# Float64 words turned into float32 with an integer add and fewer VectorE passes, in a fused attention, expert and gated feed-forward kernel

## The chip, the cores and the metric

The kernel runs on one core of one Trainium2 chip. Its time is device microseconds (us) of one launch, the median of three runs. Below, PE is the matrix engine, DVE is VectorE, ACT is ScalarE, POOL is GpSimd and SP is the engine whose queue issues the DMAs.

## The reference

Three stages follow one another, with 4 batches of 576 tokens:

```python
a = softmax(phi)                                  # (4, 8, 576, 32)
k_m, v_m = a^T k, a^T v                           # memory slots, 32 per head
attn = softmax(q k_m^T / 8) v_m                   # 8 heads of 64
x = heads side by side                            # (4, 576, 512)

out = p[e] * (relu(x @ w1[e]) @ w2[e])            # one expert e per token, 512 -> 1024 -> 512

h = relu(out @ w_in)                              # 512 -> 1024
gate = sigmoid(3-tap convolution of h along the tokens with conv_w)
result = (h * gate) @ w_out                       # 1024 -> 512
```

`w_in`, `conv_w` and `w_out` of the last stage come as float64. The host hands them over as 64-bit integers, so the kernel itself has to turn each pair of 32-bit words into one float32.

## The kernel before, in words

PE does all products as three float32 terms (high by high, high by low, low by high), so every operand is split by `split` (L144): an ACT copy (L145) writes the high part and a DVE or POOL subtraction (L146) the low part. Matmuls of this kind are written by `matmul3` (L156).

The order of the work on PE is written out by hand in `order()` (L37): per batch, 24 items, twice eight hidden tiles (`h`, matmuls into `ph`, evacuated by the ACT Relu of L599 and the DVE pass of L600) followed by four output tiles (`y`, matmuls into `py`, copied out by ACT at L650 and stored to `ydram`). Other steps hang between them: softmaxes, splits of expert weights (`wb`), the products `pv` with their split (`vh`, `vl`), routing. `ph`, `py` and others of one bank share the pool `ps1` of four banks (`bank`, L126). Only PE follows the list to the letter (`manual_schedule`, L683). The instructions of DVE, ACT and SP are put in order by a planner, which runs the program against its own estimate of times; each of these engines then takes its queue in that order and stands still when the first instruction in it has to wait.

The float64 weights go through sixteen pieces, eight of `w_in` and eight of `w_out`, of 128 partitions by 512 numbers (1024 words). `load_words` (L255) loads a piece into a tile `words` (`n0r` to `n15r`, two buffers). `narrow` (L260) takes two tiles of the tag `nar`, which has two buffers: `d` (called `nd`), which ends as the float32 result, and `t` (called `nt`), a help tile. It calls `to_f32` (L213) and then stores `nd` to `f_in` or `f_out` in device memory (L268). Only one piece is in work at a time, since its two tiles fill the tag. `narrow_next` in `order()` (L48) puts `nar.i` and behind it the load of piece i + 2 after items 4, 7, 10, 13 and 16 of batches 0 to 2, and the last after item 1 of batch 3. From batch 3 on, `f_in` is read back as the weights `wi`, and `f_out` as `wo`.

`to_f32` has two ACT passes (the absolute value of the high word into `t`, L218; the low word times 2^-52 in place, L224) and seven DVE passes: the clamp of `t` (L219), shift and mask into `nd` (L220), the top exponent bit from `t` (L221), the sign from the high word (L222), the power of two out of `nd` into `t` (L223), its product with the scaled low word (L225) and the sum (L226). L218 is kept in the order of the program against the other instructions so marked, the word loads of L258. The small table `conv_w` (24 numbers per partition) goes through the same function once (L621).

After the four batches comes `gated` (L761): per batch the products `pi` with `wi`, the convolution and the gate on DVE and ACT, and the products `po` with `wo`.

Of the kernel before, what the change touches and what calls it, by code (L numbers as in the profile page):

```python
# [6 lines left out]
F32 = mybir.dt.float32  # L7
F32R = mybir.dt.float32r
I32 = mybir.dt.int32
U32 = mybir.dt.uint32  # L10
I64 = mybir.dt.int64
AF = mybir.ActivationFunctionType
ALU = mybir.AluOpType
# [15 lines left out]
WORD_LEAST = 2.0 ** -15  # L29
WORD_MOST = float(np.array(0x47EFFFF0, np.uint32).view(np.float32))  # L30
# [82 lines left out]
def fused_kernel(tc, q, first, kv, kv_tail, phi, w1, w2, w_in, conv_w, w_out, out):  # L113
    nc = tc.nc
    wide = w_in.dtype == I64
    PSUM = bass.MemoryType.PSUM
    with (
# [92 lines left out]
        ydram = dram.tile([B, 4, 128, S], F32, name="ydram")  # L210


        def to_f32(dst, t, words, ne, first=lambda i: i):  # L213


            low, high = words[:, :, 0], words[:, :, 1]
            lowf, highf, u = low.bitcast(F32), high.bitcast(F32), dst.bitcast(I32)
            first(nc.scalar.activation(t.bitcast(F32), highf, AF.Abs))  # L218
            nc.vector.tensor_scalar(t.bitcast(F32), t.bitcast(F32), WORD_LEAST, WORD_MOST, ALU.max, ALU.min)  # L219
            nc.vector.tensor_scalar(u, t, 3, 0x3FFFFFF8, ALU.logical_shift_left, ALU.bitwise_and)  # L220
            nc.vector.scalar_tensor_tensor(u, t, 0x40000000, u, ALU.bitwise_and, ALU.bitwise_or)  # L221
            nc.vector.scalar_tensor_tensor(u, high, -0x80000000, u, ALU.bitwise_and, ALU.bitwise_or)  # L222
            nc.vector.tensor_scalar(t, u, -0x800000, None, ALU.bitwise_and)  # L223
            nc.scalar.activation(lowf, low.bitcast(U32), AF.Copy, scale=2.0 ** -52)  # L224
            ne.tensor_tensor(lowf, lowf, t.bitcast(F32), ALU.mult)  # L225
            ne.tensor_tensor(dst, dst, lowf, ALU.add)  # L226

        if wide:
            f_in = dram.tile([DM, F], F32, name="f_in")
# [4 lines left out]
        stages, staged, routed, words = [], {}, [], {}  # L234
# [13 lines left out]
        def narrow_at(i):  # L248
            if i < 8:
                at = (slice((i // 2) * 128, (i // 2) * 128 + 128), slice((i % 2) * 512, (i % 2) * 512 + 512))  # L250
                return w_in[at], f_in[at]
            at = slice((i - 8) * 128, (i - 8) * 128 + 128)
            return w_out[at, :], f_out[at, :]
# [6 lines left out]
        def narrow(i):  # L260

            if not wide:
                return
            raw = words.pop(i)
            d = fps[0].tile([128, 512], F32, tag="nar", bufs=2, name=f"nd{i}")
            t = fps[0].tile([128, 512], I32, tag="nar", bufs=2, name=f"nt{i}")
            to_f32(d, t, raw.rearrange("p (n w) -> p n w", w=2), nc.vector, tc.keep_in_program_order)
            nc.sync.dma_start(narrow_at(i)[1], d)  # L268

        def stage_w1(src, kc, name, batch=-1):  # L270
# [39 lines left out]
        def work(name, dt=F32):  # L310
            return ap.tile([128, S], dt, tag="w", bufs=5, name=name)
# [268 lines left out]
        fps = [ffn_cm.__enter__()]  # L580
# [35 lines left out]
        def conv_weights():  # L616
            dst = convw.rearrange("p k j -> p (k j)")
            if wide:
                cw_raw = work("cw_raw", I32)[:, :48]
                nc.sync.dma_start(cw_raw, conv_w.bitcast(I32))  # L620
                to_f32(dst, work("cwt", I32)[:, :24], cw_raw.rearrange("p (n w) -> p n w", w=2), nc.vector)  # L621
            else:
                nc.sync.dma_start(dst, conv_w)

# [34 lines left out]
        def gated_w(kc):  # L659
# [6 lines left out]
            "scores": scores, "gatew": gate_weights, "frow": first_row, "fcol": first_columns, "flog": first_expert, "ssoft": slot_softmax,  # L666
            "rtok": route_tokens, "rall": route_all, "rpp": route_scan, "rown": route_first, "asplit": split_attention,
            "vw": expert_vw, "vw0": lambda b: expert_vw(b, 0), "vw1": lambda b: expert_vw(b, 1), "w2": expert_w2, "nload": load_words, "nar": narrow, "win": gated_w,
            "conv": conv_weights, "close": close, "h": next_hidden, "y": next_second,
        }  # L670

# [240 lines left out]
```

## Time and profile before

| | |
|---|---|
| median of 3 runs | 458.12 us (455.39 to 459.72) |
| the profiled execution | 459.78 us |
| its span in the profile | 458.0 us, 8069 instructions |
| PE matmul busy | 418.3 us (91%) |
| PE weight loads busy | 374.8 us (82%) |
| DVE busy | 295.6 us (65%) |
| ACT busy | 222.7 us (49%) |
| POOL busy | 39.9 us (9%) |
| mean granted PE clock | 0.976 |
| mean DMA rate | 150 GB/s |

The span is cut by the profile into 40 slices; in these rows each digit is the busy share of a slice in tenths, or, for PEclk, the clock granted to PE in tenths of full speed:

```
PE   2656899998999589997999999999999999999995
DVE  2367797599865889677898767537920688057700
PEclk9996999999999979998999999999999999999999
```

Busy time of PE is modelled from the size of its matmuls, so a slice of nines need not be PE at its peak. Times below are us from the start of the span.

### The profile page before, as it was taken

The numbers are of one execution on the slowest core, as the hardware profiler recorded it, in microseconds if no ns is written. First come the engines' busy times: TensorE is split into PE (matmuls) and PEld (weight loads), VectorE is DVE, ScalarE is ACT, GpSimd is POOL, SyncE is SP. The second block draws the span as 40 slices with busy tenths as digits, with TensorE's granted clock in tenths as the row PEclk, the third lists the DMA queues.
The fourth block names the chain that finished last, engine by engine and source line by source line (L and its number), as shares of the span: only waits on it lengthen the run. The fifth ranks groups of instructions, "written<-read, shape, count | busy, mean of one in ns | idle before, by whom it ended". The sixth has DMA issues, their size and how long they took to land.

```text
span 458.0 us, 8069 instructions
## 1 busy us (share of the span) xinstructions
PE 418.3 (91%) x3202; PEld 374.8 (82%) x3203; DVE 295.6 (65%) x531; ACT 222.7 (49%) x408; POOL 39.9 (9%) x62
## 2 busy tenths in 40 slices
PE   2656899998999589997999999999999999999995
PEld 2333789977998479986999999899988998899884
DVE  2367797599865889677898767537920688057700
ACT  4235446465443543454646567157631675157511
POOL 1000000000000000000000031202420043003400
PEclk9996999999999979998999999999999999999999
DMA  8999948783595523989347100220012000100011
GB/s 251 346 336 403 359 146 295 270 260 130 189 326 167 167 83 135 355 297 390 78 163 268 41 14 3 101 92 1 0 40 76 1 2 1 69 25 1 1 72 52
DMA packets 28175, 68.77 MB, mean 150 GB/s; under 512 B 3136, under 2 KB 8000, under 8 KB 28128
## 3 DMA queue, kind: packets, MB, share of 16 engines
q1 hardware_dynamic: 28128, 68.16, 43.3%
q8 instruction: 27, 0.44, 0.4%
q14 instruction: 20, 0.16, 0.1%
HBM read 51.82 MB, written 16.33 MB: 149 GB/s over the span
## 4 chain that ended last, share of the span: by engine, by line
PE 67%; DMA 18%; DVE 10%; issue 2%; ACT 1%; SPq 1%; DVEq 0%; ACTq 0%
PE pi L156 22%; PE po L820 21%; PE py L156 14%; PE ph L156 6%; DMA f_in<-nd 4%; DMA kv<-in_kv_tail 3%; DMA f_out<-nd 3%; DMA ph<-in_phi 3%; DMA kv<-in_kv 2%; DVE wb L146 2%; DMA wb_0r<-in_w 2%; PE pk L361 1%; DMA n10r<-in_w_out 1%; DMA wa_1r<-in_w 1%; DVE vl L146 1%
## 5 line engine op out<-in xcount | busy, mean ns | idle before, releaser
L156 PEld LDWEIGHTS py<-h,wb 128*128 128x128 f32 x768 | 102.8, 188 | 8.5 <-issue 4.7
L156 PE MATMUL py<-h,wb 128*128 128x288 f32 x768 | 108.2, 298 | 1.1 <-DVE h L600 1.1
L156 PE MATMUL pi<-yh,wi 128*128 128x288 f32 x512 | 90.9, 295 | 0.0
L820 PE MATMUL po<-wo,g 128*128 128x512 f32 (+1 forms) x408 | 90.2, 377 | 0.0
L820 PEld LDWEIGHTS po<-wo,g 128*128 128x128 f32 x408 | 72.8, 188 | 13.2
L156 PEld LDWEIGHTS pi<-yh,wi 128*128 128x128 f32 x512 | 76.7, 189 | 0.9
L156 PE MATMUL ph<-att,vh 128*128 128x288 f32 x256 | 57.6, 318 | 11.4 <-ACT ys L650 6.6
L802 DVE SCALAR_TENSOR_TENSOR ct<-ht,convw,ct 128x575 f32<-128x575 f32 x32 | 29.8, 932 | 54.6 <-ACT ct L801 54.6
L156 PEld LDWEIGHTS ph<-att,vh 128*128 128x128 f32 x256 | 43.4, 201 | 17.3 <-ACT ys L650 7.1
L156 PE MATMUL pi<-yl,wi 128*128 128x288 f32 x256 | 54.9, 296 | 0.0
L786 POOL CAST tail<-g 128x128 fp32r<-128x128 f32 x32 | 21.2, 667 | 369.4 <-DVE g L146 368.8
L156 PEld LDWEIGHTS pi<-yl,wi 128*128 128x128 f32 x256 | 41.2, 188 | 0.0
L799 ACT ACTIVATE ht<-pi 128x576 f32<-128x576 f32 x32 | 20.9, 652 | 38.5 <-PE pi L156 38.5
L156 PE MATMUL ph<-att,vl 128*128 128x288 f32 x128 | 39.4, 308 | 0.0
L599 ACT ACTIVATE h<-ph 128x288 fp32r<-128x288 f32 x64 | 24.9, 406 | 24.5 <-PE ph L156 24.4
L600 DVE SCALAR_TENSOR_TENSOR h<-ph,h 128x288 fp32r<-128x288 f32 x64 | 27.3, 447 | 11.4 <-ACT h L599 11.3
L781 DVE TENSOR_TENSOR ct<-ht,ct 128x576 f32<-128x576 f32 x32 | 26.6, 830 | 8.8 <-ACT ct L780 8.6
L844 ACT ACTIVATE ot<-po 128x512 f32<-128x512 f32 x17 | 9.5, 599 | 42.0 <-PE po L820 42.0
L804 DVE SCALAR_TENSOR_TENSOR ct<-ht,convw,ct 128x575 f32<-128x575 f32 x32 | 27.3, 852 | 0.4
L145 ACT ACTIVATE g<-ct 128x576 fp32r<-128x576 f32 x32 | 21.6, 681 | 10.7 <-DVE ct L781 10.7
L156 PEld LDWEIGHTS ph<-att,vl 128*128 128x128 f32 x128 | 25.8, 201 | 0.0
L801 ACT ACTIVATE ct<-ht,convw 128x576 f32<-128x576 f32 x32 | 24.7, 771 | 0.4
(247 smaller groups left out, 510.9 us busy)
## 6 DMA issues: line engine op xcount, KB each, us to landing
kv<-in_kv SPq DMA_DIRECT2D x8, 1024.0 KB, 12.1
q<-in_q SPq DMA_DIRECT2D x8, 576.0 KB, 9.3
ydram<-ys SPq DMA_DIRECT2D x32, 144.0 KB, 2.4
y<-ydram SPq DMA_DIRECT2D x4, 1152.0 KB, 5.9
out<-ot SPq DMA_DIRECT2D x15, 256.0 KB, 2.2
ph<-in_phi SPq DMA_DIRECT2D x8, 288.0 KB, 10.2
adram<-at SPq DMA_DIRECT2D x8, 288.0 KB, 7.7
wa_0r<-in_w SPq DMA_DIRECT2D x4, 512.0 KB, 4.1
```

The lines of the kernel that those rows point to most:

```text
L145: nc.scalar.activation(hi, src, AF.Copy)
L146: (eng or nc.vector).tensor_tensor(lo, src, hi.bitcast(F32), ALU.subtract)
L156: nc.tensor.matmul(ps, st, mv[:, cols], start=i == 0, stop=i == len(terms) - 1)
L599: nc.scalar.activation(t[:, 0, :], ps, AF.Relu)
L600: nc.vector.scalar_tensor_tensor(t[:, 1, :], ps, 0.0, t[:, 0, :].bitcast(F32), ALU.max, ALU.subtract)
L781: slow(f"gm.{f}").tensor_tensor(ct, ht, ct, ALU.mult)
L786: nc.gpsimd.tensor_copy(tail[:, f, :, to:to + 64], t[:, :, 512:576].bitcast(F32))
L799: nc.scalar.activation(two(ht), halves(ps), AF.Relu)
L801: nc.scalar.activation(ct, ht, AF.Copy, scale=convw[:, 1, f:f + 1])
L802: nc.vector.scalar_tensor_tensor(ct[:, 1:], ht[:, :S - 1], convw[:, 0, f:f + 1], ct[:, 1:], ALU.mult, ALU.add)
L804: nc.vector.scalar_tensor_tensor(ct[:, :S - 1], ht[:, 1:], convw[:, 2, f:f + 1], ct[:, :S - 1], ALU.mult, ALU.add)
L820: nc.tensor.matmul(ps[:, cols], st[sp], w[:, mp, f % 2, cols], start=f == 0 and i == 0, stop=f == 7 and i == 2)
```

## The change

`to_f32` keeps two ACT passes and has four DVE passes in place of seven. The absolute value now goes into the result tile `dst` itself. The low word is scaled by 2^-29 and written by ACT as an integer of a few bits into a tile `r` of its own (it was scaled in place in the word tile). DVE clamps `dst`, shifts and masks it, takes two bits (sign and top exponent bit) from the high word in one pass, and adds `r` as an integer. `narrow` still takes two tiles of the tag `nar`, the second now called `nl`; `conv_weights` is changed alike. The diff, whole but for context:

```diff
-        def to_f32(dst, t, words, ne, first=lambda i: i):
+        def to_f32(dst, r, words, first=lambda i: i):
             low, high = words[:, :, 0], words[:, :, 1]
-            lowf, highf, u = low.bitcast(F32), high.bitcast(F32), dst.bitcast(I32)
-            first(nc.scalar.activation(t.bitcast(F32), highf, AF.Abs))
-            nc.vector.tensor_scalar(t.bitcast(F32), t.bitcast(F32), WORD_LEAST, WORD_MOST, ALU.max, ALU.min)
-            nc.vector.tensor_scalar(u, t, 3, 0x3FFFFFF8, ALU.logical_shift_left, ALU.bitwise_and)
-            nc.vector.scalar_tensor_tensor(u, t, 0x40000000, u, ALU.bitwise_and, ALU.bitwise_or)
-            nc.vector.scalar_tensor_tensor(u, high, -0x80000000, u, ALU.bitwise_and, ALU.bitwise_or)
-            nc.vector.tensor_scalar(t, u, -0x800000, None, ALU.bitwise_and)
-            nc.scalar.activation(lowf, low.bitcast(U32), AF.Copy, scale=2.0 ** -52)
-            ne.tensor_tensor(lowf, lowf, t.bitcast(F32), ALU.mult)
-            ne.tensor_tensor(dst, dst, lowf, ALU.add)
+            u = dst.bitcast(I32)
+            first(nc.scalar.activation(dst, high.bitcast(F32), AF.Abs))
+            nc.scalar.activation(r, low.bitcast(U32), AF.Copy, scale=2.0 ** -29)
+            nc.vector.tensor_scalar(dst, dst, WORD_LEAST, WORD_MOST, ALU.max, ALU.min)
+            nc.vector.tensor_scalar(u, u, 3, 0x3FFFFFF8, ALU.logical_shift_left, ALU.bitwise_and)
+            nc.vector.scalar_tensor_tensor(u, high, -0x40000000, u, ALU.bitwise_and, ALU.bitwise_or)
+            nc.vector.tensor_tensor(u, u, r, ALU.add)
...
             d = fps[0].tile([128, 512], F32, tag="nar", bufs=2, name=f"nd{i}")
-            t = fps[0].tile([128, 512], I32, tag="nar", bufs=2, name=f"nt{i}")
-            to_f32(d, t, raw.rearrange("p (n w) -> p n w", w=2), nc.vector, tc.keep_in_program_order)
+            r = fps[0].tile([128, 512], I32, tag="nar", bufs=2, name=f"nl{i}")
+            to_f32(d, r, raw.rearrange("p (n w) -> p n w", w=2), tc.keep_in_program_order)
...
-                to_f32(dst, work("cwt", I32)[:, :24], cw_raw.rearrange("p (n w) -> p n w", w=2), nc.vector)
+                to_f32(dst, work("cwl", I32)[:, :24], cw_raw.rearrange("p (n w) -> p n w", w=2))
```

## Rows read from the trace of the kernel before

**Rows 1.** Stretches: length; PE, PEld, DVE, ACT, POOL busy us (instructions); clock; DMA.

```profile
51.00:154.00 103.00, 99.95 (x971) 89.52 (x970) 81.78 (x172) 50.84 (x108) 0.00 (x0) 1.00 0.68 230
154.00:160.00 6.00, 0.95 (x7) 0.50 (x5) 4.47 (x7) 2.92 (x5) 0.00 (x0) 0.94 0.53 157
160.00:166.00 6.00, 4.81 (x29) 3.27 (x30) 4.45 (x10) 2.54 (x7) 0.00 (x0) 0.50 0.19 66
209.00:214.00 5.00, 1.91 (x12) 1.45 (x11) 4.13 (x8) 3.12 (x7) 0.00 (x0) 0.99 1.03 410
214.00:218.00 4.00, 4.00 (x22) 3.94 (x22) 1.91 (x6) 1.13 (x3) 0.00 (x0) 0.58 0.79 305
218.00:450.00 232.00, 232.00 (x1460) 215.53 (x1459) 137.46 (x190) 119.69 (x193) 38.30 (x44) 1.00 0.16 53
```

**Rows 2.** What PE waited for from 51 to 218: us, times, longest.

```profile
PE ph L156 <- ACT ys L650: 6.6, 2, 5.0
PE ph L156 <- DVE fw L432: 2.4, 2, 1.2
PE ph L156 <- DVE h L600: 2.3, 2, 1.5
PE py L156 <- DVE h L600: 1.1, 2, 0.6
```

**Rows 3.** The chain of waits across the longest of them: start, us, what.

```profile
153.64 0.32 SPq L268
...
154.01 4.75 DMA n10r<-in_w_out
...
159.42 0.39 ACT ys L650
```

**Rows 4.** Groups of instructions by line, four DVE passes: busy us, mean ns | idle before.

```profile
L221 DVE SCALAR_TENSOR_TENSOR nd<-nt,nd 128x512 int32<-128x512 int32 x16 | 10.9, 681 | 0.1
L220 DVE TENSOR_SCALAR nd<-nt 128x512 int32<-128x512 int32 x16 | 6.7, 421 | 15.3 <-DMA f_in<-nd 12.0 <-DMA f_out<-nd 3.3
L219 DVE TENSOR_SCALAR nt<-nt 128x512 f32<-128x512 f32 x16 | 6.7, 417 | 0.1
L223 DVE TENSOR_SCALAR nt<-nd 128x512 int32<-128x512 int32 x16 | 6.6, 414 | 0.2
```

**Rows 5.** Instructions of the word tile of piece 0: ns shortest/median/longest, start us.

```profile
L224 ACT ACTIVATE n0r<-n0r x1: 668/668/668, 44.9 to 44.9; 128x512 f32<-128x512 uint32 x1
...
L225 DVE TENSOR_TENSOR n0r<-n0r,nt x1: 681/681/681, 64.0 to 64.0; 128x512 f32<-128x512 f32 x1
L226 DVE TENSOR_TENSOR nd<-nd,n0r x1: 669/669/669, 66.0 to 66.0; 128x512 f32<-128x512 f32 x1
```

**Rows 6.** Groups of instructions by line, one twice as wide.

```profile
L146 DVE TENSOR_TENSOR vl<-pv,vh 128x1024 fp32r<-128x1024 f32 x8 | 9.7, 1218 | 2.4 <-ACT vh L145 2.4
```

**Rows 7.** ACT's waits before L224 (first, last of ten) and before L218: us, times.

```profile
DVE nd L221: 5.1, 2
...
DMA n14r<-in_w_out: 1.1, 1
...
DVE n13r L225: 2.1, 1
```

**Rows 8.** Stores of L268, from issue to landing.

```profile
DMA to landing us min/median/max: 2.0/3.6/11.2
```

**Rows 9.** Timeline of SP, ACT and DVE around the store of piece 6: start, us, instruction.

```profile
129.97 0.51 SPq L268 DMA_DIRECT2D f_in<-nd  x1
...
131.08 0.41 ACT L599 ACTIVATE h<-ph 128x288 fp32r<-128x288 f32 x1 [0.60 <-PE ph L156]
...
135.70 0.41 ACT L599 ACTIVATE h<-ph 128x288 fp32r<-128x288 f32 x1 [0.71 <-PE ph L156]
...
139.49 0.43 DVE L220 TENSOR_SCALAR nd<-nt 128x512 int32<-128x512 int32 x1 [4.09 <-DMA f_in<-nd]
139.83 0.45 DVE L600 SCALAR_TENSOR_TENSOR h<-ph,h 128x288 fp32r<-128x288 f32 x1
```

## The prediction

> **What bounds the kernel now.** I read the mean clock and the page's slices first, then the busy times by stretch, what PE waited for, the chain of waits, and last the timelines of ACT, DVE and SP around the longest waits. From 218 us to 450 us PE is busy without a gap at full clock [rows 1]. Nothing in that half can be gained by a lighter DVE, and no conversion but the last lies in it. Before 51 us PE waits for the first loads and the softmaxes. What the change can reach lies between 51 and 218 us, where fifteen of the sixteen pieces are converted.
>
> There PE stands still for 103.00 - 99.95 = 3.05 us up to 154, for 5.05 in 154 to 160, for 1.19 in 160 to 166 and for 3.09 in 209 to 214, in all 12.4 us [rows 1]; the list of its waits has the same sum [rows 2]. After the two longest gaps the clock falls: 4.81 us of busy time ran at 0.50, which is the 1.2 GHz level, and 4.00 us at a mean of 0.58 [rows 1]. At full clock these would have taken 2.4 and 1.7 us less. So 12.4 + 4.1 = 16.5 us is the most that can be had.
>
> All of these waits end with ACT or DVE [rows 2]. The longest shows why [rows 3]: piece 8 leaves DVE, its store is issued at 153.64, behind it the load of piece 10 at 154.01, which takes 4.75 us. In ACT's queue L224 of piece 10 stands ahead of the copy `ys`, which empties a PSUM bank, so that copy starts at 159.42 and PE has no bank until then. A late conversion thus stops PE by way of ACT's queue. The second long wait of PE for `ys`, 6.6 - 5.0 = 1.6 us, is of the same kind: L218 of piece 14 waited 2.1 us there for L225 of piece 13 [rows 7].
>
> **The change part by part.** The DVE passes L221 (0.68), L223 (0.41) and one of the two-tensor passes (L225, 0.68) go: 1.78 us per piece [rows 4, 5]. What stays is 0.42 + 0.42 + 0.68 + 0.67 = 2.19 of 3.97 us (the pass that takes bits from the high word costs what L221, of its kind, costs). Over fifteen pieces DVE has 26.7 us less to do between 51 and 218 us. That is not 26.7 us off the time: PE sets the end, and only the waits counted above can shrink.
>
> The last pass is new in type: two int32 tensors added. Its bounds are 0.41 (an int32 pass with one tensor, L223) and 1.22 (a two-tensor pass of twice the width [rows 6]); I take 0.67, the row of the same shape in float32 [rows 5]. At 1.22 the saving per piece would be 1.23 in place of 1.78 us, and at 0.41 it would be 2.04. ACT keeps two passes. The second now writes integers into another tile; I take L224's 0.67 [rows 5], and between half and twice that it moves ACT by -0.3 to +0.7 us per piece, which its idle half has room for (50.84 busy in 103 us [rows 1]). The small table `conv_w` loses three passes of about 0.15 us each, beside other work: nothing.
>
> Two waits move. First, L224 worked in place and needed only its words, so the planner put it early in ACT's queue, ahead of the words' arrival: ACT stood 24.6 us before it in all, ten causes from 5.1 down to 1.1 us [rows 7]. Now that pass writes `nl`, whose buffer the piece before holds until its last DVE pass or its store is done. Those come a whole piece after the words were asked for, so the words have landed, and this kind of wait goes. Second, the wait for the store of the piece before (it must have read `nd`) stood on DVE ahead of L220, 15.3 us in all [rows 4]. As both tiles of a piece share two buffers, one of the two ACT passes takes it over now. Behind it in ACT's queue are the Relus (L599), the `ys` copies and the splits. A landing takes 3.6 us in the middle and 11.2 at worst [rows 8]. In the longest of these waits, 4.09 us, ACT had run six Relus before DVE's wait ended [rows 9]. Had they stood behind it, PE would have stopped; as it was, ACT had nothing to do just then. The wait costs between nothing (ACT idle, as in most of the places where L220 now waits) and some 20 us (worked out with the rivals); I take 1.5 us: about 0.7 where the last Relu of a half comes late, the rest for splits pushed back.
>
> The loop of one piece gets shorter. It was landing, then L220 to L226 (0.42 + 0.68 + 0.68 + 0.41 + 0.68 + 0.67 = 3.5 us), then the store; it is landing, one or two ACT passes of 0.67, four DVE passes of 2.2. That is 0.0 to 0.7 us less, and DVE is free for the splits while it waits.
>
> The sum, gap by gap. The waits for `fw` are 2.4 us in two, of which 1.19 stand behind the long gap and 1.2 at 104 us [rows 1, 2]. So the 3.05 us before 154 are 1.9 up to 59 us, where DVE is behind because of a late load of `phi`: that stays. At 104 DVE comes late to `fw` through a full queue (81.78 of 103 us busy [rows 1]); with two pieces' 3.6 us less in front of it that gap goes. The gap of 5.05 shrinks to 0.4, since piece 8 leaves DVE 3 us earlier (its own 1.78 and a split of 1.22 [rows 6] that DVE can take while it waits) and no load stands ahead of `ys`. The 1.19 behind it goes, and so do the 2.4 of the slow clock, as short gaps elsewhere left the clock at 1.00. Of the 3.09 + 1.7 around 212 I count half, 2.4, as that place hangs on the store too. In all 1.2 + 4.65 + 1.19 + 2.4 + 2.4 = 11.8, less 1.5 for the moved wait: 10.3 us.
>
> Made against the profiled execution, 459.78 - 10.3 = 449.5 us. The median of the runs is 1.7 us lower, which gives 447.8. I say 449.0.
>
> A rule that speaks against it: PE's share is 91% of the span and DVE's 65%, and between 51 and 154 us DVE has 81.78 busy us of 103, ACT 50.84 and PE 99.95 [rows 1]. The Trainium skill (Perfetto Trace Analysis, Identifying the Most-Contended Engine) says to optimize the engine with the highest occupancy first, and by it DVE work taken away here is worth nothing: about 458 us. The rows on the gaps differ, since it is a queue's order and not its sum that stops PE, and the sum by them is the 10.3 us above.
>
> **The rivals.** *No change: late inputs change their names.* ACT still runs a queue made from estimated times, and each of its two passes still has a late input, the last DVE pass or the store of the piece before. L218 has waits of the first kind now, as the 2.1 us ahead of piece 14 [rows 7]. If `ys` meets such a wait in the same place, the 5.05 us and the slow clock behind it stay, and only 1.2 and the 2.4 around 212 go: 459.8 - 3.6 = 456 us. For it speaks that waits on ACT, not DVE's sum, made the longest gap; against it, that the words have landed by then and the stores mostly land in 3.6 us.
>
> *Slower: the store's wait stops the Relus.* Two stores are long, that of piece 1 (11.2 us [rows 8]) and that of piece 6 (issued 129.97, over at 139.49 [rows 9]), and both run while PE does hidden tiles, each of which needs a Relu. If the waiting ACT pass stands ahead of the Relus, the one of 131.08 starts near 140.1. PE's lead through four banks is about 2.4 us (0.8 us a tile), so it stands 9.0 - 2.4 = 6.6 us, and the slow clock adds 2.4 as it did at 160: 9.0. For piece 1, with 11.2 us in place of 9.5, it is about 10.5. With both, 449.5 + 19.5 = 469 us; with one, 459, no change. So it decides from two such places on. Against it: the planner put L220, with the same wait, behind all but one of the DVE passes of those Relus [rows 9]. The Trainium skill (TensorE: Matmul & The Clock Gate, on the array's architecture and the queue depths) calls ACT's and DVE's queues strictly first in, first out; rows 3 agree, as `ys` could not pass L224.
>
> *Faster still: all gaps from 104 us on go.* Then 16.5 - 1.9 = 14.6 us: 445 us, or 443.5 against the median.
>
> *The change does not save what it says.* With an integer add of 1.22 us, DVE saves 18.5 in place of 26.7 us; the gap at 104 and half of the one at 212 would stay, 453 us.
>
> **How the numbers follow.** The forecast has 0.45, the faster case 0.10, the dear add 0.05, no change 0.25 and the slower case 0.15. A measurement of this kernel tells about 1% from no change, here 4.6 us. Below 453.5 us lie the first two and a part of the third: 0.57. Within 1% I put 0.27 (no change, one stopped stretch), above 462.7 us 0.16 (two stopped stretches, or a worse order of the queues). The range runs from 442.0, all gaps gone, to 464.0, past one stopped stretch: it leaves out less than 0.05 below and about 0.13 above. The forecast's own range is 445 to 453.
>
> **What would show it.** Right, step by step: four DVE passes per piece with about 2.2 us busy and an add near 0.67; DVE busy near 267 us; no idle time of ACT ending with a load of words from piece 2 on; idle time of ACT ending with `f_in<-nd` and `f_out<-nd` or the last DVE pass, under 20 us; no gap of PE over 2 us after 60 us and no stretch below full clock after 51; and the full stretch of PE beginning about 10 us earlier. Wrong: a gap of PE that ends with a Relu or a `ys` held behind a store; an add of over 1 us; or gaps in places where there were none, by a new order on DVE and ACT.

## The result, and the profile after

The changed kernel takes 445.73 us (median of 4 runs, 443.41 to 446.40); the kernel before, now with 4 runs, 457.28. The ratio is 0.9735 with a 95% interval of 0.9674 to 0.9797. The profiled execution took 446.12 us against 459.78, that is 13.66 us less. The prediction, 449.0 with 442.0 to 464.0, contains the time, and its sum of 10.3 us was 3.4 us short for the profiled execution.

The busy times of the page, changed kernel:

```profile
span 444.1 us, 8032 instructions
PE 414.5 (93%) x3202; PEld 372.9 (84%) x3203; DVE 272.2 (61%) x480; ACT 220.8 (50%) x408; POOL 41.9 (9%) x62
```

PE and ACT run as many instructions as before; DVE has 51 fewer, three for each of the sixteen pieces and for `conv_w`, and is busy 23.4 us less. The stretches that answer to [rows 1] (columns as there):

```profile
51.00:104.00 53.00, 51.92 (x487) 46.62 (x485) 37.19 (x75) 28.77 (x58) 0.00 (x0) 0.97 0.76 268
104.00:150.00 46.00, 45.94 (x460) 41.07 (x460) 31.94 (x71) 22.41 (x52) 0.00 (x0) 1.00 0.70 238
150.00:205.00 55.00, 54.51 (x453) 50.17 (x452) 45.59 (x98) 31.80 (x62) 0.00 (x0) 1.00 0.69 239
205.00:436.00 231.00, 231.00 (x1453) 214.63 (x1452) 131.62 (x176) 116.58 (x190) 40.25 (x44) 1.00 0.17 56
```

PE now stands still for 1.08 + 0.06 + 0.49 = 1.6 us after 51, against 12.4 before, and its unbroken stretch begins at 205, not 218. What PE waited for from 48 to 220 us, answering to [rows 2] (us in total, times, longest; L597 is the old L600, L429 the old L432):

```profile
PE py L156 <- DVE h L597: 1.1, 2, 0.5
PE ph L156 <- DVE h L597: 0.3, 1, 0.3
PE ph L156 <- DVE fw L429: 0.2, 1, 0.2
```

The waits for `ys`, 6.6 us, are gone, and no wait behind a Relu took their place. Three of the four DVE passes, answering to [rows 4, 5]:

```profile
L223 DVE CUSTOM_DVE_ANT_0 nd<-nd,nl 128x1024 uint16<-128x1024 uint16 x16 | 11.0, 686 | 5.4 <-ACT nl L219 5.2
L220 DVE TENSOR_SCALAR nd<-nd 128x512 f32<-128x512 f32 x16 | 6.8, 424 | 5.1 <-ACT nd L218 4.9
L221 DVE TENSOR_SCALAR nd<-nd 128x512 int32<-128x512 int32 x16 | 6.6, 412 | 0.1
```

No DVE pass waits for a store any more (15.3 us before). ACT's pass over the low word does. What it waited for, and, in the last row, what the stores took to land:

```profile
DMA f_in<-nd: 8.1, 4
DMA f_out<-nd: 5.2, 3
...
DMA to landing us min/median/max: 2.0/3.5/9.2
```

Not one wait of ACT for words of a piece is left. How a piece now goes is seen on piece 4, whose predecessor's store is issued at 86.36. ACT's timeline (start, us, instruction):

```profile
86.37 0.67 ACT L218 ACTIVATE nd<-n4r 128x512 f32<-128x512 f32 x1 [0.66 <-DVE nd L223]
89.27 0.41 ACT L647 ACTIVATE ys<-py 128x288 f32<-128x288 f32 x1 [2.23 <-DMA f_in<-nd]
89.58 1.05 ACT L145 ACTIVATE wb<-wb_0r 128x1024 fp32r<-128x1024 f32 x1
90.53 0.67 ACT L219 ACTIVATE nl<-n4r 128x512 int32<-128x512 uint32 x1
```

and DVE's:

```profile
87.07 0.43 DVE L220 TENSOR_SCALAR nd<-nd 128x512 f32<-128x512 f32 x1 [0.73 <-ACT nd L218]
87.53 0.43 DVE L221 TENSOR_SCALAR nd<-nd 128x512 int32<-128x512 int32 x1
87.99 0.69 DVE L222 SCALAR_TENSOR_TENSOR nd<-n4r,nd 128x512 int32<-128x512 int32 x1
...
91.80 0.69 DVE L223 CUSTOM_DVE_ANT_0 nd<-nd,nl 128x1024 uint16<-128x1024 uint16 x1
```

`nd` takes the buffer that `nl` of the piece before has left, so three of the four DVE passes run while that piece's store is still on its way. Only the low word (L219), and behind it the add, waits for the landing. So the passes behind the landing went from six (3.5 us, L220 to L226 of before) to one ACT and one DVE pass. The last store of a piece is issued at 204.30 us; in the kernel before it was at 242.28.

### The profile page after: what moved, and what is told of

It is laid out like the page before. It is cut to its first block, busy times and chain, and to the rows that moved or that the text cites. A ratio compares the mean times of both kernels' runs of the same rounds, so it can differ in the third digit from the quotient of the medians.

```text
span 444.1 us, 8032 instructions
## 1 busy us (share of the span) xinstructions
PE 414.5 (93%) x3202; PEld 372.9 (84%) x3203; DVE 272.2 (61%) x480; ACT 220.8 (50%) x408; POOL 41.9 (9%) x62
## 4 chain that ended last, share of the span: by engine, by line
PE 84%; DMA 8%; DVE 4%; ACT 1%; issue 1%; SPq 1%; ACTq 0%
PE pi L156 23%; PE py L156 23%; PE po L817 22%; PE ph L156 9%; DMA ph<-in_phi 6%; DMA kv<-in_kv 2%; PE pl L471 2%; PE pk L358 2%; PE pv L380 1%; PE sc L380 1%; DVE nm L330 1%; DVE h L597 1%; DVE wb L146 1%; ACT wb L145 0%; PE pa L344 0%
## 5 line engine op out<-in xcount | busy, mean ns | idle before, releaser
L156 PEld LDWEIGHTS py<-h,wb 128*128 128x128 f32 x768 | 104.3, 191 | 8.1 <-issue 3.9
L156 PE MATMUL py<-h,wb 128*128 128x288 f32 x768 | 109.6, 300 | 1.1 <-DVE h L597 1.1
L783 POOL CAST tail<-g 128x128 fp32r<-128x128 f32 x32 | 23.0, 720 | 359.4 <-DVE g L146 358.6
L156 PE MATMUL ph<-att,vh 128*128 128x288 f32 x256 | 54.9, 307 | 0.6 <-DVE h L597 0.3
L156 PEld LDWEIGHTS ph<-att,vh 128*128 128x128 f32 x256 | 41.5, 192 | 5.2 <-issue 1.7
L156 PE MATMUL ph<-att,vl 128*128 128x288 f32 x128 | 38.3, 299 | 0.0
L597 DVE SCALAR_TENSOR_TENSOR h<-ph,h 128x288 fp32r<-128x288 f32 x64 | 27.6, 448 | 8.7 <-ACT h L596 8.6
L778 DVE TENSOR_TENSOR ct<-ht,ct 128x576 f32<-128x576 f32 x32 | 27.7, 866 | 7.1 <-ACT ct L777 7.1
L647 ACT ACTIVATE ys<-py 128x288 f32<-128x288 f32 x32 | 13.0, 406 | 32.5 <-issue 15.4
L798 ACT ACTIVATE ct<-ht,convw 128x576 f32<-128x576 f32 x32 | 24.6, 769 | 0.3
```

The costliest lines, as they stand in the source:

```text
L156: nc.tensor.matmul(ps, st, mv[:, cols], start=i == 0, stop=i == len(terms) - 1)
L597: nc.vector.scalar_tensor_tensor(t[:, 1, :], ps, 0.0, t[:, 0, :].bitcast(F32), ALU.max, ALU.subtract)
L647: nc.scalar.activation(yt, ps, AF.Copy)
L778: slow(f"gm.{f}").tensor_tensor(ct, ht, ct, ALU.mult)
L783: nc.gpsimd.tensor_copy(tail[:, f, :, to:to + 64], t[:, :, 512:576].bitcast(F32))
L798: nc.scalar.activation(ct, ht, AF.Copy, scale=convw[:, 1, f:f + 1])
```

## The experiments

Two things went at once: DVE passes, and what stands behind a store or ahead of a load. The first theory, that of the prediction, was that PE's gaps came from ACT standing ahead of words that had not landed ("queue"); its rival was that DVE's work itself is the gain ("work"). All times are medians, ratios are against the kernel before on the same chip (459.2 to 459.7 us there); the range in brackets is the 95% interval of the ratio.

**e1: the low word taken out of its early place in ACT's queue (kernel before).**

```diff
             first(nc.scalar.activation(t.bitcast(F32), highf, AF.Abs))
+            first(nc.scalar.activation(lowf, low.bitcast(U32), AF.Copy, scale=2.0 ** -52))
...
-            nc.scalar.activation(lowf, low.bitcast(U32), AF.Copy, scale=2.0 ** -52)
```

> The kernel before, with all its seven VectorE passes and its tiles; only the ACT pass over the low word (L224) is queued right behind L218 of its own piece, so that it no longer stands early in ACT's queue ahead of the load of its words. Theory 'queue' (PE's gaps came from ACT standing ahead of words that had not landed): the gap of 5.05 us at 154, the 1.19 and the slow clock behind it go (8.6 us), the gap at 104 and those at 212 (L218 waiting for L225) stay: 449 us, between 446 and 452 against 457.3. Theory 'work' (the 26.7 us of VectorE passes are the gain): 457 us, within 2. In the trace by 'queue': no idle time of ACT over 1 us that ends with a load of words.

455.07 us, ratio 0.989 (0.982 to 0.996): some 4 or 5 us, half of what "queue" said. Its waits of PE from 48 to 220 us:

```profile
PE ph L156 <- DVE fw L432: 4.9, 2, 3.3
PE py L156 <- DVE h L600: 1.6, 3, 0.6
PE ph L156 <- DVE h L600: 1.5, 1, 1.5
PE ph L156 <- ACT ys L650: 1.4, 1, 1.4
```

The waits for words and the gap of 5.05 us are gone, as expected; but at the same place PE now waits for DVE, 3.35 us until its next matmul at 157.96. DVE's timeline there:

```profile
152.51 0.43 DVE L221 TENSOR_SCALAR nd<-nt 128x512 int32<-128x512 int32 x1 [0.58 <-DMA f_out<-nd]
...
156.50 1.22 DVE L146 TENSOR_TENSOR wb<-wb_3r,wb 128x1024 fp32r<-128x1024 f32 x1
157.63 0.27 DVE L432 SCALAR_TENSOR_TENSOR fw<-pfa,other 8x128 f32<-8x128 f32 x1
```

The passes of piece 9 start when the store of piece 8 has landed, and `fw` stands behind them and behind the split `wb_3`. The early pass was one form of the trouble, not its cause.

**e2: three DVE passes left out, all else as before.**

```diff
-            nc.vector.scalar_tensor_tensor(u, t, 0x40000000, u, ALU.bitwise_and, ALU.bitwise_or)
...
-            nc.vector.tensor_scalar(t, u, -0x800000, None, ALU.bitwise_and)
...
-            ne.tensor_tensor(lowf, lowf, t.bitcast(F32), ALU.mult)
```

> The kernel before without L221, L223 and L225: four VectorE passes per piece, so the conversion is left incomplete and the output is not the reference's; the low word is still scaled in place and early in ACT's queue, and the store's wait is still VectorE's. Theory 'work': 446 us, as the changed kernel. Theory 'queue': ACT still stands ahead of the words, though they are asked for 1.8 to 3 us earlier per piece, so the gap at 154 shrinks from 5 to 2 or 3 us and the slow clock may stay: 451 to 455 us.

447.11 us, ratio 0.9735 (0.967 to 0.980): the whole gain, while ACT still stands waiting ahead of words. The first, second and last of ten causes before its pass over the low word (L222 here):

```profile
DMA n10r<-in_w_out: 2.7, 1
DMA n5r<-in_w_in: 2.6, 1
...
DMA n13r<-in_w_out: 1.1, 1
```

Summed over the ten, that is 19.8 us, all of it for words. Of the 24.6 us before [rows 7], 5.1 were waits for DVE and 19.5 were for words. So the waits for words are as long as before, and yet PE's waits behind ACT in this kernel came to 0.2 us: by themselves these waits do not make the gaps, and "queue" falls as their cause.

**e3: the changed kernel with seven passes.** The values stay the same.

```diff
+            nc.vector.tensor_scalar(dst, dst, WORD_LEAST, WORD_MOST, ALU.max, ALU.min)
...
+            nc.vector.scalar_tensor_tensor(u, high, -0x40000000, u, ALU.bitwise_and, ALU.bitwise_or)
+            nc.vector.scalar_tensor_tensor(u, high, -0x40000000, u, ALU.bitwise_and, ALU.bitwise_or)
```

> The changed kernel with the clamp done twice and the bit pass three times: the same values, but seven VectorE passes per piece (0.42 + 0.68 + 0.68 = 1.78 us more each, 28 us in all, as before). ACT's passes and the tiles stay as changed. Theory 'queue': words are no longer waited for, so most of the gain stays: 447 to 451 us. Theory 'work': the gain is gone, 455 to 459 us.

449.66 us, ratio 0.977 (0.970 to 0.984), with DVE busy 296.9 us to the end of its work, as much as before. "Work" falls too: most of the gain is there without any pass saved. So either part alone brings most of the gain or all of it, and both together no more than e2.

**A new theory, "late pieces".** The conversions run as one chain: store of a piece, landing, what stands behind the landing, next store. When this chain is slower than PE's list, pieces come later than the planned queues of DVE and ACT have them, and they hold up what stands behind them there: `fw`, `h` or `ys`. Both parts of the change shorten that chain. Three kernels (e5, e6, e7) were made to tell this from "amount" (DVE's sum).

**e5: the two ACT passes swapped, so that all four DVE passes stand behind the landing.**

```diff
-            first(nc.scalar.activation(dst, high.bitcast(F32), AF.Abs))
-            nc.scalar.activation(r, low.bitcast(U32), AF.Copy, scale=2.0 ** -29)
+            first(nc.scalar.activation(r, low.bitcast(U32), AF.Copy, scale=2.0 ** -29))
+            first(nc.scalar.activation(dst, high.bitcast(F32), AF.Abs))
```

> The changed kernel with its two ACT passes swapped, both kept in order: the low word first, so that it takes the buffer that comes free first, and the absolute value waits for the store of the piece before. All four VectorE passes then stand behind that store, not the add alone. Theory 'late pieces' (PE's gaps come when conversions fall behind PE's list; what sets their pace is the store's landing and the passes that stand behind it): 1.5 us more per piece on that path, still below before's 3.5, so a little slower than the changed kernel: 446 to 449 us. Theory 'amount' (only the sum of VectorE's work counts): 445.7, within 1.5.

445.88 us, ratio 0.968 (0.962 to 0.974): no difference from the changed kernel. It doesn't tell the two theories apart.

**e6: the swap of e5 with the seven passes of e3.**

> The swap of e5 together with the seven passes of e3: the same VectorE work as e3 (449.7), but all seven passes stand behind the store of the piece before, as six did in the kernel before. Theory 'late pieces': the gain of e3 is lost for the most part: 454 to 458 us. Theory 'amount': as e3, 448 to 451 us. Theory 'words' (what mattered was that no ACT pass stands ahead of a load of words): as e1 or e3, 449 to 455 us.

454.76 us, ratio 0.988 (0.981 to 0.994). The sum of DVE's work is that of e3, and 5 us of e3's gain are gone, by the order of two ACT passes alone (and the queues that the planner made for it). e3 and e6 ran on two chips and their intervals overlap a little (0.981 to 0.984), but the fastest run of e6 (452.37) is slower than the slowest of e3 (450.91). The range of "words" (449 to 455) holds this time too; e7 tells that theory apart. Its waits of PE, from 48 to 220 us:

```profile
PE ph L156 <- DVE fw L432: 5.1, 2, 2.8
PE py L156 <- DVE h L600: 1.5, 3, 0.6
PE py L156 <- ACT h L599: 0.7, 1, 0.7
```

**e7: the kernel before with three buffers for the tag `nar`.**

```diff
-            d = fps[0].tile([128, 512], F32, tag="nar", bufs=2, name=f"nd{i}")
-            t = fps[0].tile([128, 512], I32, tag="nar", bufs=2, name=f"nt{i}")
+            d = fps[0].tile([128, 512], F32, tag="nar", bufs=3, name=f"nd{i}")
+            t = fps[0].tile([128, 512], I32, tag="nar", bufs=3, name=f"nt{i}")
...
```

The lines left out drop the tile of ones, which made the room; where it was read, the identity or a tile set to one on the spot stands in.

> The kernel before with three buffers of the tag nar in place of two (the tile of ones dropped for room): seven passes, the low word early in ACT's queue as before, but no pass waits for the store of the piece before. Theory 'late pieces': the pieces no longer fall behind, most of the gain comes without any change to the passes: 447 to 451 us. Theory 'amount': 457 to 459 us, as before.

450.96 us, ratio 0.980 (0.972 to 0.988), with nothing of the arithmetic touched and all seven passes in place: near e3, and not the 457 to 459 of "amount". "Words" falls as well: ACT still waits for words, 20.1 us between 48 and 220 against 17.5 in the kernel before.

**e4 and e11: the changed kernel with three buffers.**

> The changed kernel with three buffers of the tag nar in place of two (the tile of ones is dropped for room; nothing else changes), so that no ACT pass has to wait for the store of the piece before: the 13.3 us of ACT's waits for stores go. If these waits are harmless, as PE's list of waits has none behind them: 445.7 within 2 us. If they still cost by pushing back splits and copies: 440 to 443 us.

> e4 again, beside the changed kernel on the same chip: if the waits for the store are harmless, within 1.5 us of e10; if they cost, 2 to 4 us below it.

444.46 us (ratio 0.964), and again 445.50 (0.971). **e10** is the changed kernel in the same call as e11.

> The changed kernel itself, beside the runs of this call, as their measure: 445.7 within 1.5 us.

It took 447.73 us (445.45 to 447.97), ratio 0.976, which is 2.0 above the 445.7 and so outside the 1.5 us expected; e11 took 443.87 to 447.88. By the words of the expectation e11, 2.2 us below e10, fell to "they cost", and e4 to "harmless". The medians can't decide it: the runs overlap, and so do the intervals (0.964 to 0.979 for e11, 0.968 to 0.983 for e10). The traces say more. ACT's 13.3 us of waits for stores are gone in e4 and e11, but PE's idle time between 51 and 220 us is 1.16 and 1.02 us there, against 1.63 and 1.26 in the two profiles of the changed kernel. And the profiled executions of e10, e4 and e11, in each of which PE's clock fell twice (see the end), have the same span: 446.0, 446.0 and 446.1 us. So the moved wait costs PE at most some 0.6 us, and the third buffer is no proven better version. e4 and e11 drop the tile of ones as e7 does, with nothing clear gained by it, so e7's gain is hardly from there.

**e8 and e9: five and six passes behind the landing**, from e5 with the bit pass, and then the clamp too, done twice.

> e5 with the bit pass done twice: five VectorE passes behind the store of the piece before, 0.68 us more per piece. If the time follows the pieces' pace evenly between e5 (445.9, four passes, 2.2 us) and e6 (454.8, seven passes, 4.0 us): 449 us. If there is a threshold, pieces keeping up with PE's list up to some pace: 446 to 447 us and the last store near 215 us, not past 230.

> e5 with the bit pass and the clamp done twice: six passes behind the store, 1.1 us more per piece. Even slope: 451 us. Threshold between five and seven: either 447 with the last store before 225, or 453 to 455 with the last store past 235.

451.93 us (0.987, 0.983 to 0.991) and 450.83 (0.984, 0.976 to 0.991). e9 is on the 451 of the even slope, but e8 lies 3 us above its 449 and its last store is past 230, so neither form of expectation fits both. By the medians the fifth pass costs 6 us, the sixth nothing and the seventh 4; only the first of these is clear of the intervals (e5 ends at 0.974, e8 begins at 0.983; e8, e9 and e6 overlap). Each edit also makes the planner lay out new queues, so a pass has no fixed price here.

The kernels in the order of their last store, which tells how late the pieces are, with PE's idle time from 51 to 220 us (169.00 less its busy time) in the profiled execution, the median time and the ratio:

| kernel | last store issued, us | PE idle, us | time, us | ratio |
|---|---|---|---|---|
| e2, three passes out | 202.42 | 3.01 | 447.1 | 0.974 |
| changed | 204.30 | 1.63 | 445.7 | 0.974 |
| e10, changed again | 206.22 | 1.26 | 447.7 | 0.976 |
| e4, changed, three buffers | 206.22 | 1.16 | 444.5 | 0.964 |
| e11, the same again | 206.29 | 1.02 | 445.5 | 0.971 |
| e5, changed, ACT passes swapped | 211.00 | 2.57 | 445.9 | 0.968 |
| e7, before, three buffers | 215.72 | 6.08 | 451.0 | 0.980 |
| e3, changed, seven passes | 216.47 | 4.52 | 449.7 | 0.977 |
| e8, five behind the landing | 231.87 | 5.01 | 451.9 | 0.987 |
| e9, six behind the landing | 233.45 | 7.70 | 450.8 | 0.984 |
| e1, low word later | 236.98 | 9.38 | 455.1 | 0.989 |
| before | 242.28 | 12.38 | 457.3 | 1 |
| e6, seven behind the landing | 268.0 | 7.36 | 454.8 | 0.988 |

Where the last store is issued by 211 us, the ratio is 0.964 to 0.976; between 215 and 234, 0.977 to 0.987; past 236, 0.988 and more. The order is not strict: e6 is by far the latest and not the slowest, and neighbours in the table can't be told apart. Lateness is thus shown as what the kernels with and without the gain differ in, and e7 (a buffer) and e6 against e3 (an order of two passes) set it by one edit each. What one late piece costs is not shown: it depends on what stands behind it in that kernel's queues.

## Why the prediction was right

The time, the sign and the place were right: the gain lies between 51 and 218 us, in PE's gaps, and the half behind it is unchanged. The reason given for the longest gap was not the one that the runs bear out, so that part of the agreement is luck. By its steps:

- **Passes.** 2.19 us per piece were expected; 0.42 + 0.41 + 0.68 + 0.69 = 2.20 were measured. The add took 0.69, near the 0.67 taken. DVE's busy time fell by 23.4 us (to 272.2), not 28 (to 267): the 28 was a sum of durations, and in the records one instruction can start before the last has ended (on ACT above, 89.27 + 0.41 = 89.68, and the next starts at 89.58), so that a sum of durations is more than the busy time. The two traces hold the 4.6 us: the durations of the passes on `nd` and `nt` or `nl` fell by 28.3 us in sum, as expected, those of all DVE instructions by 27.4 (324.4 to 297.0), and the time that is counted twice in that sum fell from 28.8 to 24.8.
- **Waits for words.** They went, as said, though only 19.5 of the 24.6 us taken for them were waits for words. But the step "a late conversion thus stops PE by way of ACT's queue" failed as the cause: with these waits gone and the passes kept (e1) some 4 us came, against the 8.6 that the sum had given to this gap and its slow clock, and with the waits kept and three passes gone (e2) all of it came. In the place of that step stands the pace of the chain of pieces, which both parts of the change shorten (e3, e6, e7). The sentence on this gap has that in part, "piece 8 leaves DVE 3 us earlier", but as one piece's own saving. What a piece saves adds up from piece to piece: the store of piece 8 is issued at 138.69 us in the changed kernel and at 153.64 before, 15 us earlier.
- **The loop of one piece.** It was taken as 0.0 to 0.7 us shorter, with all four passes behind the landing. In fact one of the four is, since `nd` takes the free buffer. That was missed, though the text saw that either ACT pass might get the wait. e5 shows that at four passes it does not matter, e6 that at seven it does.
- **The moved wait.** 13.3 us of waits on ACT against 15.3 on DVE before. PE's idle time shows at most some 0.6 us of cost (e4, e10 and e11), so the 1.5 us taken for it was too much as far as the traces tell, and the slower rival, Relus held behind a store, did not come.
- **The sum.** The gaps at 104, 154 and 161 went as said. The place around 212, counted at half, went whole (+2.4), the moved wait cost PE next to nothing (+1.5), and the gaps before 59 us fell from 1.9 to 1.1 (+0.8). Against it stands one fall of the clock, told below (-1.7); "no stretch below full clock after 51" was among the signs and failed by it. That is 10.3 + 3.0 = 13.3 of the 13.66 us measured. So with the gaps it was the rival "faster still", at 0.10, that came (445 us for the profiled execution, which took 446.12 with the fall of the clock in it), and the median of 445.73 lies at the lower edge of the forecast's own 445 to 453.
- **The rule on the most contended engine** (the Trainium skill, Perfetto Trace Analysis, Identifying the Most-Contended Engine). The section says which engine to optimize first; that work taken from another is worth nothing was the prediction's reading of it. It also has PE judged by the arithmetic it does as a share of its peak, or by its weight loads' busy share, and not by its matmuls'. Here the weight loads' share is 82% in place of 91%, above DVE's 65% either way. The measured ratio is against the prediction's reading: DVE was not the busiest engine, and e2, which takes passes from DVE alone, has the whole gain. What decided was when its work came. The page's next section, Optimization Strategy, says to find the gaps of the engine that one optimizes and what blocks it there, and fits this case better.

## What to carry to other kernels

Where a side job runs as a chain through small buffers, look at what stands behind each landing, not at the sum of its engine: three passes fewer brought some 12 us here (e2), a buffer more some 9 without them (e7), and the order of two instructions decided over 5 (e3 and e6). And before a gap is put down to the wait that ends last, take that wait away alone: in e1 another wait came up in the same place. A useful sign of such a chain is the time at which its last member ends, compared with the place that the written order gives it.

## What was not expected of the hardware

The add of two int32 tensors appears in the records as an instruction of its own, `CUSTOM_DVE_ANT_0`, on 128x1024 elements of uint16, and takes 686 ns, as long as a float32 pass with two tensors of 512 elements (669 and 681 ns [rows 5]). Writing int32 from ACT costs what float32 does: 0.66 to 0.70 us.

PE's clock fell without a gap. In the changed kernel (columns as in [rows 1]):

```profile
82.00:84.00 2.00, 2.00 (x25) 2.00 (x24) 0.67 (x2) 0.41 (x1) 0.00 (x0) 1.00 1.06 416
84.00:86.00 2.00, 2.00 (x13) 2.00 (x13) 0.36 (x1) 0.77 (x2) 0.00 (x0) 0.67 1.02 418
86.00:88.00 2.00, 2.00 (x10) 2.00 (x10) 1.20 (x4) 0.67 (x1) 0.00 (x0) 0.50 1.03 341
88.00:90.00 2.00, 2.00 (x17) 2.00 (x17) 0.68 (x1) 0.73 (x2) 0.00 (x0) 0.98 0.98 317
```

What PE had done just before (timeline):

```profile
82.30 2.13 PE L471 MATMUL pl<-vwg,at 128*96 128x9 f32 x24
84.28 8.00 PE L156 MATMUL py<-h,wb 128*128 128x288 f32 x47
```

PE was busy all the time by the records, but with 24 matmuls of nine columns each for 2.1 us; behind them the granted clock was at 0.50, the 1.2 GHz level, until 88. It costs 2.00 x 0.33 + 2.00 x 0.50 = 1.7 us. In the kernel before, the same matmuls were followed by full clock (1.00 from 80 to 110), so they alone do not bring it about; what does was not tried.

Nor does the fall belong to the change. PE does the same 24 matmuls for each batch, in this profile also at 62.59 and at 134.53 us, and there the clock stayed at 1.00. In e10, the same kernel profiled again, it fell behind the first group as well as behind the second (timeline and stretches, in order of time):

```profile
62.74 2.21 PE L471 MATMUL pl<-vwg,at 128*96 128x9 f32 x24
66.00:68.00 2.00, 2.00 (x11) 2.00 (x10) 2.00 (x6) 0.27 (x1) 0.00 (x0) 0.50 0.02 7
84.03 2.15 PE L471 MATMUL pl<-vwg,at 128*96 128x9 f32 x24
86.00:88.00 2.00, 2.00 (x10) 2.00 (x10) 0.26 (x1) 0.77 (x2) 0.00 (x0) 0.50 1.03 424
```

The profiled execution of e10 took 447.97 us, that of the changed kernel 446.12: about one such fall apart. So two medians of this kernel that are 2 us apart say little until their clocks have been compared.
